# W's even rows in DMAs of 16 partitions instead of one of 64, and two pieces of the start's loads re-queued

## The chip, the cores and the metric

One NeuronCore of a Trainium2 chip runs the whole program. The metric is device time in microseconds (us). A time is the median of several executions; a run is called slow when it is over 1.5% above the fastest of the same kernel. "Span" is the profiled part of one execution; here it is about 1.7 us shorter than the time of that execution. A DMA is a transfer that the DMA engines carry out after some engine has issued it; "issued" and "landed" are the times of its issue and of the last increment of its semaphore in the trace. A call is one set of runs on one chip; the calls used different chips.

## The reference

Two branches of the same x [2048, 512] are mixed by a gate. Branch a is a spectral filter, branch b a two-layer network with Mish.

```python
x = A_x
g = sigmoid((x * gate_w).sum(-1, keepdims=True))
a = irfft2(rfft2(x) * (w_r + 1j * w_i))          # w_r, w_i: [2048, 257]
b = einsum(mish(einsum(x, w1) + b1), w2)         # w1: [512, 1792], w2: [1792, 512]
return g * a + (1 - g) * b
```

## The kernel before

The kernel is a list of tasks (one group of matmuls, one eviction, one DMA) that a list scheduler in the kernel file puts into one fixed order per engine when the program is built. In this program each engine then works through its own list in that order and waits at semaphores where it needs another's result.

TensorE's work, roughly in order: warm matmuls on zeros, transposes of x (L586), two stages of the spectral transform (L625, L636) interleaved with the first layer (L821, `mm1`), then the second layer (L843, `mm2`), the spectral middle with W (L761, L790), and the inverse stages (L870, L888). Between the stages the spectral data goes through DRAM twice: "shuffle writes" (`scr<-R`) and "shuffle reads" (`R<-scr`). The tile called hsb holds Mish results, and at first also the raw W (`SW`).

```python
def dma(name, dst, src, nbytes, reads=(), writes=(), deps=(), ..., queue="sp", ...):   # L465 is the issue
    ...
NWARM = 15
dma("ld_b1", ..., queue="act")
ld_x(0, 2); ld_w1(0); ld_x(2, 4); ld_w1(1)        # x on SyncE's queue; w1 pieces 0 and 1 on ScalarE's
ld_c(0, ...); ld_w1(2); ld_x(4, 8); ...           # SyncE's queue

def wload(w, src_t, deps=()):                     # w_r: 0, w_i: 1
    S_ = SW[:, w, :, :]
    row = S_.ap[0][0]
    G_ = (128 * 257, 16)
    # even partitions: 64 partitions, each one run of 16*257 elements (8224 bytes)
    S2 = bass.AP(S_.tensor, S_.offset, [[2 * row, 64], [1, 16 * 257]])
    part(0, S2, src(0, (16 * 257, 4), G_, (1, 16 * 257)), 64 * 8224, 300e3)   # source: 4 x 16 x 4112
    # odd partitions: 16 partitions each, rows of 257 elements (514 bytes), in reverse
    for bb in (0, 2, 1, 3):
        part(1 + bb, dst(...), src(..., G_, (-257, 16 - e0), (1, 257)), ...)
    part(5, ...)

wload(0, A_w_r)
ld_w2(0)
... # first stages; the four shuffle writes r1w
wload(1, A_w_i, t_e2)                             # t_e2: the evictions of L636
dma("ld_sm", SM[:], ...)                          # constants of the spectral middle
ld_w2(1, t_e2)
... # eight shuffle reads r1r
```

## Time and profile before

| | before |
|---|---|
| time, median of 3 | 141.91 us (141.03 to 142.57) |
| span of the profiled execution | 142.1 us |
| TensorE busy | 127.5 us, 90% |
| VectorE, ScalarE busy | 68%, 63% |

The execution that was profiled took 143.79 us, 1.9 more than this median.

From the page of the kernel before: span, TensorE's busy time, and three rows that cut the span into 40 slices of 3.55 us (busy share of TensorE, granted TensorE clock, busy share of the DMA engines, all in tenths).

```profile
span 142.1 us, 2309 instructions
PE 127.5 (90%) x800; PEld 68.4 (48%) x814; DVE 96.7 (68%) x213; ACT 89.0 (63%) x146; POOL 4.3 (3%) x8
...
PE   6574899999999906999999999999999999999992
...
PEclk9999999999999997799999999999999999999999
DMA  3999937999942896973446007210399722221021
```

TensorE is full from the sixth slice to the last, but for one hole (the 0 and the 6 near 50 us). In the slice of the 6 and in the one after it the clock is down to seven tenths. From 39 to 46 us, ahead of the hole, the DMA engines are only four and two tenths busy.

The waits of TensorE in the kernel before (what it waited for: total us, times, longest):

```profile
PE ps L843 <- DMA w_sb<-in_B_w_dram: 4.6, 1, 4.6
PE ps L821 <- DMA w_sb<-in_B_w_dram: 4.1, 2, 2.2
PE ps L508 <- DVE GD L505: 1.1, 1, 1.1
```

The hole is a wait for w2 (4.6 us). The 4.1 us are two waits for pieces of w1 at the start. TensorE's timeline shows where the hole falls: the second layer starts with w2's first half, and the second half is needed after 28 matmuls (one record is missing in the trace):

```profile
43.73 6.21 PE L843 MATMUL ps<-w_sb,hsb 128*128 128x512 bf16 x27
54.58 4.88 PE L843 MATMUL ps<-w_sb,hsb 128*128 128x512 bf16 x14 [4.65 <-DMA w_sb<-in_B_w_dram]
```

The timeline of SyncE's DMA queue in the kernel before (start us, length us of the issues, what, count):

```profile
16.18 6.10 SPq L465 DMA_DIRECT2D hsb<-in_A_w_r_dram  x6
22.32 1.49 SPq L465 DMA_DIRECT2D w_sb<-in_B_w_dram  x1
23.86 5.32 SPq L465 DMA_DIRECT2D SM<-c_sm  x1
29.36 4.00 SPq L465 DMA_DIRECT2D scr<-R  x4
33.41 11.81 SPq L465 DMA_DIRECT2D hsb<-in_A_w_i_dram  x6
45.27 0.59 SPq L465 DMA_DIRECT2D w_sb<-in_B_w_dram  x1
46.87 12.66 SPq L465 DMA_DIRECT2D R<-scr  x8
```

The six w_i issues took 11.81 us, although most issues take 0.6 to 0.8 us: the last one alone took 7.77 us. Only then, at 45.27 us, could w2's second half be issued. It landed at 54.54 us.

Windows of the kernel before (stretch; then TensorE busy, its weight loads, VectorE, ScalarE, GpSimd; last three columns: granted clock, DMA share, GB/s; the share adds up the times of packets, and these overlap, so it passes 1: 1.20 in the last row):

```profile
40.00:44.00 4.00, 4.00 (x21) 1.82 (x19) 3.80 (x10) 3.12 (x6) 1.78 (x1) 1.00 0.28 106
44.00:50.00 6.00, 5.88 (x27) 2.49 (x26) 5.40 (x10) 4.49 (x3) 1.74 (x1) 1.00 0.68 170
50.00:56.00 6.00, 1.42 (x5) 0.61 (x6) 2.96 (x5) 3.41 (x2) 0.00 (x0) 0.93 0.78 172
56.00:60.00 4.00, 4.00 (x15) 1.60 (x14) 0.28 (x1) 1.65 (x3) 0.00 (x0) 0.68 1.20 233
```

In 40 to 44 us the DMA share is 0.28, about 4 engines of 16, while a load that TensorE needs has not even been issued. That fits a transfer that uses few engines.

### The profile page before, as it was taken

To read this page: it belongs to the slowest core of one execution; us is meant where nothing else is said; L and a number is where in the kernel's file an instruction comes from. 1 tells how busy PE (TensorE), PEld (TensorE's weight loads), DVE (VectorE), ACT (ScalarE), POOL (GpSimd) and SP (SyncE) were. 2 spreads that over 40 slices of the span, in tenths; PEclk is the share of its full clock that TensorE was granted. 3 is DMA by queue.
4 is the path that set the end of the run, shared out by engine and by line. 5 is a ranking of instruction groups with operands and counts; after the bars stand their busy time and mean duration, and the time that the engine had idled before them with its cause. 6 is when DMAs were issued, how large, how long until landed. Compare 5 with 4: busy or idle time off the path is not lost.

```text
span 142.1 us, 2309 instructions
## 1 busy us (share of the span) xinstructions
PE 127.5 (90%) x800; PEld 68.4 (48%) x814; DVE 96.7 (68%) x213; ACT 89.0 (63%) x146; POOL 4.3 (3%) x8
## 2 busy tenths in 40 slices
PE   6574899999999906999999999999999999999992
PEld 4354767664444402444344354444445665665451
DVE  0512849779999835199999999995003899799422
ACT  0333987998888728436495878896886665875000
POOL 2000000000018000000000000000000000000000
PEclk9999999999999997799999999999999999999999
DMA  3999937999942896973446007210399722221021
GB/s 101 322 401 405 257 90 115 166 175 326 392 151 95 212 213 152 227 123 86 99 109 187 1 0 294 105 51 24 141 237 217 123 91 110 95 81 74 2 109 37
DMA packets 33136, 22.01 MB, mean 155 GB/s; under 512 B 24037, under 2 KB 29413, under 8 KB 32997
## 3 DMA queue, kind: packets, MB, share of 16 engines
q1 hardware_dynamic: 32040, 21.35, 57.9%
q10 hardware_dynamic: 1084, 0.53, 1.3%
q8 instruction: 6, 0.10, 0.3%
q14 instruction: 6, 0.04, 0.1%
HBM read 14.00 MB, written 6.29 MB: 143 GB/s over the span
## 4 chain that ended last, share of the span: by engine, by line
PE 47%; DVE 21%; DMA 14%; SPq 8%; issue 4%; ACT 3%; ACTq 1%; DVEq 0%
PE ps L843 20%; PE ps L821 16%; DMA w_sb<-in_B_w_dram 14%; SPq L465 8%; DVE PX L775 4%; DVE PX L774 4%; DVE PX L771 3%; DVE PX L778 3%; PE ps L888 3%; PE ps L870 3%; ACT R L491 2%; DVE R L490 2%; PE ps L625 2%; DVE WW L669 2%; PE ps L636 1%
## 5 line engine op out<-in xcount | busy, mean ns | idle before, releaser
L843 PE MATMUL ps<-w_sb,hsb 128*128 128x512 bf16 (+2 forms) x231 | 52.6, 375 | 5.0 <-DMA w_sb<-in_B_w_dram 4.6
L821 PE MATMUL ps<-xT,w_sb 128*128 128x512 bf16 (+1 forms) x233 | 52.8, 369 | 4.9 <-DMA w_sb<-in_B_w_dram 4.1
L830 ACT ACTIVATE hsb<-ps,b1f 128x512 bf16<-128x512 f32 (+1 forms) x60 | 38.4, 662 | 11.1 <-PE ps L821 11.0
L843 PEld LDWEIGHTS ps<-w_sb,hsb 128*128 128x128 bf16 x238 | 22.7, 100 | 29.2 <-DMA w_sb<-in_B_w_dram 5.1
L821 PEld LDWEIGHTS ps<-xT,w_sb 128*128 128x128 bf16 x240 | 23.0, 99 | 28.1 <-issue 2.6
L490 DVE CAST R<-ps 128x512 bf16<-128x512 f32 (+1 forms) x22 | 14.6, 687 | 7.6 <-PE ps L625 5.7
L491 ACT ACTIVATE R<-ps 128x512 bf16<-128x512 f32 (+1 forms) x26 | 14.5, 594 | 4.2 <-PE ps L625 2.5
L854 ACT ACTIVATE R<-ps,omg 128x512 bf16<-128x512 f32 x12 | 8.2, 686 | 8.5 <-PE ps L843 8.5
L491 ACT ACTIVATE PX<-ps 128x512 bf16<-128x512 f32 x15 | 8.9, 595 | 4.7 <-DVE PX L775 2.3
L666 ACT ACTIVATE WW<-hsb 32x2080 bf16<-32x2080 bf16 x4 | 7.8, 1938 | 4.1 <-DMA hsb<-in_A_w_i_dram 3.8
L665 DVE COPY WW<-hsb 32x2080 bf16<-32x2080 bf16 x12 | 8.4, 696 | 2.7 <-DMA hsb<-in_A_w_i_dram 2.4
L677 DVE SCALAR_TENSOR_TENSOR R<-R,gwb 128x512 bf16<-128x512 bf16 x16 | 9.9, 685 | 0.3 <-ACT R L491 0.3
L895 ACT ACTIVATE PX<-ps,gcol 128x256 f32<-128x256 f32 x14 | 6.3, 472 | 4.6 <-PE ps L888 4.6
L877 DVE CAST TT<-ps 128x512 bf16<-128x512 f32 x3 | 2.0, 688 | 9.9 <-PE ps L870 9.9
L778 DVE TENSOR_TENSOR PX<-PX 128x512 bf16<-128x512 bf16 x16 | 6.8, 423 | 0.8
L880 ACT ACTIVATE TT<-ps 128x512 bf16<-128x512 f32 x13 | 7.3, 595 | 0.0
L774 DVE TENSOR_TENSOR PX<-PX,WW 64x512 bf16<-64x512 bf16 x16 | 6.7, 421 | 0.5
L775 DVE TENSOR_TENSOR PX<-PX,WW 64x512 bf16<-64x512 bf16 x16 | 6.7, 419 | 0.2
L771 DVE TENSOR_TENSOR PX<-PX,WW 128x512 bf16<-128x512 bf16 x16 | 6.7, 420 | 0.2
L916 DVE SCALAR_TENSOR_TENSOR R<-ps,omg,R 128x512 bf16<-128x512 f32 (+2 forms) x5 | 3.2, 642 | 4.9 <-PE ps L843 4.9
L904 DVE SCALAR_TENSOR_TENSOR PX<-ps,gcol,PX 128x256 bf16<-128x256 f32 x12 | 5.7, 478 | 0.7 <-ACT PX L895 0.7
L790 PE MATMUL ps<-PX,SM 128*128 128x512 bf16 x15 | 5.7, 382 | 0.4 <-DVE PX L778 0.3
(72 smaller groups left out, 97.8 us busy)
## 6 DMA issues: line engine op xcount, KB each, us to landing
scr<-R SPq DMA_DIRECT2D x8, 512.0 KB, 6.8
R<-scr SPq DMA_DIRECT2D x16, 256.0 KB, 5.0
w_sb<-in_B_w_dram SPq DMA_DIRECT2D x2, 896.0 KB, 11.6
out_dram<-R SPq DMA_DIRECT2D x7, 256.0 KB, 2.0
R<-in_A_x_dram SPq DMA_DIRECT2D x3, 512.0 KB, 10.7
w_sb<-in_B_w_dram SPq DMA_DIRECT2D x1, 1280.0 KB, 8.9
hsb<-in_A_w_r_dram SPq DMA_DIRECT2D x1, 514.0 KB
hsb<-in_A_w_i_dram SPq DMA_DIRECT2D x1, 514.0 KB
```

Source lines behind the costliest of these rows:

```text
L465: start = (lambda e: e.dma_start_transpose(dst, src)) if transpose else (lambda e: e.dma_start(dst, src))
L490: t = G.add(name, [("dve", dve_dur(n), lambda e: e.tensor_copy(out=outf(), in_=inf())), ("act", act_dur(n), lambda e: e.activation(outf(), ...
L491: ("act", act_dur(n), lambda e: e.activation(outf(), inf(), AF.Copy))],
L665: t_wc.append(G.add(f"wv{w}{bb}{v}", [("dve", dve_dur(2080, 4), lambda e, wv=wv: e.tensor_copy(**wv())), ("act", act_dur(2080), lambda e, ...
L677: t_gx.append(G.add(f"gx{t}", [("dve", 0.72, lambda e, t=t: e.scalar_tensor_tensor(out=x_sb[:, t, :], in0=x_sb[:, t, :], scalar=1.0, in1=g ...
L771: return e.tensor_tensor(out=v(P1, sP, 0, 128), in0=v(Xb, sX, 0, 128), in1=Wa[:, js, 0:128], op=ALU.mult)
L774: e.tensor_tensor(out=v(P2, sQ, 0, 64), in0=v(Xb, sX, 64, 128), in1=Wb[64:128, js, 0:128], op=ALU.mult)
L775: return e.tensor_tensor(out=v(P2, sQ, 64, 128), in0=v(Xb, sX, 0, 64), in1=Wb[0:64, js, 0:128], op=ALU.mult)
L778: return e.tensor_tensor(out=P1[:, sP.i, :], in0=P1[:, sP.i, :], in1=P2[:, sQ.i, :], op=ALU.add)
L821: ins = e.matmul(ps[:, bk(sl), cols], w1_sb[:, dt_, 128 * ft:128 * (ft + 1)], xT[:, dt_, 4 * c + h0:4 * c + h1, :], start=(dt_ == 0), stop ...
L830: return e.activation(hsb[:, hb, ft, cols], ps[:, bk(sl), cols], AF.Mish, bias=b1f[:, ft:ft + 1])
L843: ins = e.matmul(ps[:, bk(sl), 0:n1 - n0], hsb[:, hb, ft, 128 * tl:128 * (tl + 1)], w2_sb[:, ft, n0:n1], start=(ft == 0), stop=(ft == NFT ...
```

## The change

Its intent: W's even rows should use all DMA engines; w1's second piece should not be late; the constants should not stand ahead of the first shuffle's writes. Numbers of the scheduler's model were changed as well, so the order of all engines was computed anew. Cut to its core:

```diff
-NWARM = 15
+NWARM = 20
-XBAR_BW = 95e3
+XBAR_BW = 270e3
...
-            t = G.add(name, [(queue, {"sp": 0.46, "act": 0.46, "pool": 1.0}[queue], start)],
+            t = G.add(name, [(queue, 1.3 if transpose else 0.46, start)],
...
-            ... queue="act" if h < 2 else "sp", prio=199.5 - 2 * h if h < 2 else None)
-
-        dma("ld_b1", ..., queue="act", prio=202.0)
-        ld_x(0, 2, bw=400e3)
+            ... queue="sp" if h else "act", prio=None if h else 199.5)
+
+        ld_x(0, 2, bw=250e3)
         ld_w1(0)
-        ld_x(2, 4)
+        dma("ld_b1", ..., queue="act", prio=198.5)
+        G.tasks[-1].lat = 0.8
+        ld_x(2, 4, bw=290e3)
         ld_w1(1)
...
-            S2 = bass.AP(S_.tensor, S_.offset, [[2 * row, 64], [1, 16 * 257]])
-            part(0, S2, src(0, (16 * 257, 4), G_, (1, 16 * 257)), 64 * 8224, 300e3)
             for bb in (0, 2, 1, 3):
                 e0 = 0 if bb else 1
+                part(6 + bb, bass.AP(S_.tensor, S_.offset + 32 * bb * row, [[2 * row, 16], [1, 16 * 257]]), src(16 * bb, G_, (1, 16 * 257)), 16 * 8224, 220e3)
                 part(1 + bb, dst(32 * bb + 1, 16, e0, 16 - e0), ...)
...
         wload(1, A_w_i, t_e2)
-        dma("ld_sm", SM[:], ...)
         ld_w2(1, t_e2)
+        dma("ld_sm", SM[:], ..., deps=t_e2)
```

More of the change, by code (lines that the diff above doesn't have):

```diff
@@ L209 @@
     __slots__ = ("name", "opts", "eng", "dur", "fn", "deps", "pools", "prio", "idx", "isdma", "xfer",
-                 "sem", "semval", "sig", "start", "done", "nleft", "succ", "bias")
+                 "lat", "sem", "semval", "sig", "start", "done", "nleft", "succ", "bias")
 class _Slot:
@@ L248, in add @@
         t.isdma = False
-        t.xfer = t.bias = 0.0
+        t.xfer = t.bias = t.lat = 0.0
         t.sem, t.semval, t.sig = None, 0, 0
@@ L356, in schedule @@
                 bw_free = xs + t.xfer
-                t.done = bw_free + 0.9
+                t.done = bw_free + 0.9 + t.lat
             else:
@@ L520, in ld_w1 @@
         def ld_w1(h):
-            f0, f1, bw = ((0, 256, 250e3), (256, 512, 280e3), (512, F, 370e3))[h]
-            dma(f"ld_w1_{h}", w1_sb[:, :, f0:f1], w1v[:, :, f0:f1], 128 * 4 * 2 * (f1 - f0), writes=[("w1", h)], bw=bw, queue="act" if h < 2 else "sp", prio=199.5 - 2 * h if h < 2 else None)
-        dma("ld_b1", bgraw[0:14, :], B_b1.rearrange("(ft p) -> ft p", p=128), 3584, writes=["braw"], queue="act", prio=202.0)
-        ld_x(0, 2, bw=400e3)
+            f0, f1, bw = ((0, 256, 290e3), (256, 512, 290e3), (512, F, 370e3))[h]
+            dma(f"ld_w1_{h}", w1_sb[:, :, f0:f1], w1v[:, :, f0:f1], 128 * 4 * 2 * (f1 - f0), writes=[("w1", h)], bw=bw, queue="sp" if h else "act", prio=None if h else 199.5)
+        ld_x(0, 2, bw=250e3)
         ld_w1(0)
-        ld_x(2, 4)
+        dma("ld_b1", bgraw[0:14, :], B_b1.rearrange("(ft p) -> ft p", p=128), 3584, writes=["braw"], queue="act", prio=198.5)
+        G.tasks[-1].lat = 0.8
+        ld_x(2, 4, bw=290e3)
         ld_w1(1)
@@ L649, in _build @@
         wload(1, A_w_i, t_e2)
-        dma("ld_sm", SM[:], d_c["SM"][:], 128 * 2 * 128 * len(MATS), writes=["SM"])
         ld_w2(1, t_e2)
+        dma("ld_sm", SM[:], d_c["SM"][:], 128 * 2 * 128 * len(MATS), writes=["SM"], deps=t_e2)
         t_wc = []
@@ L666, in _build @@
                                             ("act", act_dur(2080), lambda e, wv=wv: e.activation(wv()["out"], wv()["in_"], AF.Copy))],
-                          reads=[("S", w, 0), ("S", w, 1 + bb)] + [("S", w, 5)] * (not bb), writes=[("W", w, v, bb)], deps=t_e2, prio=PR["cp"]))
+                          reads=[("S", w, 6 + bb), ("S", w, 1 + bb)] + [("S", w, 5)] * (not bb), writes=[("W", w, v, bb)], deps=t_e2, prio=PR["cp"]))
             for h in range(2):
```

## The prediction

> **What bounds it now.** TensorE: the page's first part has it 90% busy (127.5 of 142.1 us), and the timeline shows dense matmuls from 12.7 us to 139.4 us with one hole. The waits view names its idle time: 4.6 us for w2's second half (the hole, 49.9 to 54.6 us), 4.1 us for two pieces of w1 at the start (2.2 us up to 8.0, 1.9 us up to 12.7), 1.1 us for the first memset. After the hole the granted clock is 0.68 in 56 to 60 us (windows view; the clock records have one half-speed stretch of 3.4 us), so about 1.7 us more are lost there.
>
> **Why the hole.** Each W load starts with one DMA whose source has an outer dimension of 4. [...] that DMA's semaphore gets four late increments (30.6 to 30.9 us for w_r, 47.2 to 49.0 for w_i). Every later transfer shows 12 increments early and 4 late: w2's first half 30.9 to 32.1 against 36.0 to 36.2 us, the w_i pieces 38 to 40 against 47 to 52. The mean DMA share meanwhile is 0.28 to 0.45 (40 to 48 us). SyncE's queue stalls behind it: one w_i issue took 7.77 us (37.5 to 45.3), so w2's second half was issued only at 45.3 and landed at 54.5; the shuffle reads ran 46.9 to 63.1.
>
> **The change.** The 514 KB DMA becomes four of 16 partitions, which should use all 16 engines. It costs 6 more issues at 0.6 to 0.9 us on SyncE's queue, which has the time. Expected order: last shuffle write, nine w_i DMAs, w2's second half, constants, eight shuffle reads. Estimate: last shuffle write issued near 32 us, nine issues of 0.7 us to 38.3, w2's second half landed near 42 to 43 us, constants near 44, shuffle reads (1.2 us each, as now) done near 53 to 54 instead of 63. TensorE needs the second half at about 48: the hole (4.65) and its slow clock (1.7) go. Gate products and W copies keep VectorE until about 54, so its middle phase ends near 89 instead of 97, and the second shuffle moves with it.
>
> At the start, w1's second piece on ScalarE's queue landed on its last engine at 12.6 us although half had landed at 8.3; behind x 2-3 on SyncE's queue it should land near 7 to 8. b1 behind w1's first piece costs nothing (first use 9 us). The 1.9 us wait goes; the 2.2 us one shrinks by 0 to 1; five more warm matmuls fill idle time. Estimate 2 us.
>
> **Sum.** 142 - 4.65 - 1.7 - 2 = 133.6 us; I add 1.4 us for new small waits in the fixed order: 135.0 us, range 132.3 to 138.8. Chances: faster 0.88, same 0.10, slower 0.02.
>
> **What would show it.** No 4-late pattern in W's landings; no issue over 3 us after 30 us; no TensorE wait on w2 over 1 us; full clock in 50 to 60 us; first shuffle's reads done by 55; no w1 wait near 12 us; TensorE's busy share 93 to 95%.
>
> **What would make it wrong.** The shuffle reads overtake w2's second half (the hole stays); a shuffle write waiting on SyncE holds up W's pieces; short rows set W's time; VectorE's middle phase becomes the limit and TensorE waits for it or for the second shuffle.

142 - 4.65 - 1.7 - 2 = 133.6, and 1.4 for new waits, make the 135.0 us. That DMAs of 16 partitions would use all 16 engines was only my expectation then; what the runs show of it stands below, under "How many engines a DMA used".

## The result

| | before | after |
|---|---|---|
| time, median of 4 | 141.47 us (140.75 to 142.57) | 133.12 us (133.04 to 133.44) |
| span of the profiled execution | 142.1 us | 131.7 us |
| TensorE busy | 127.5 us, 90% | 126.1 us, 96% |
| w2's second half issued / landed | 45.27 / 54.54 us | 33.58 / 42.55 us |
| first matmul of the second layer | 43.73 us | 39.39 us |
| first shuffle's reads done | 63.07 us | 53.73 us |

The kernel is faster: ratio 0.9408, 95% interval 0.9338 to 0.9477. A ratio here is the mean time of one kernel's fast runs over that of the other's of the same rounds, so it is not quite the ratio of the medians.

The page of the kernel after, the same rows (slices of 3.29 us):

```profile
span 131.7 us, 2348 instructions
PE 126.1 (96%) x819; PEld 67.9 (52%) x819; DVE 94.9 (72%) x211; ACT 90.3 (69%) x149; POOL 4.3 (3%) x8
...
PE   6998999999999999999999999899999999999991
...
PEclk9999999999999999999999999999999999999999
DMA  3999989999999999134493212039992224002211
```

TensorE is full from the second slice on, the hole and the low clock are gone, and the DMA engines are busy almost without a break until 53 us. TensorE's waits after (the same view; the three longest):

```profile
PE ps L508 <- DVE GD L505: 1.1, 1, 1.1
PE ps L636 <- ACT R L491: 0.6, 1, 0.6
PE ps L790 <- DVE PX L778: 0.5, 1, 0.5
```

No wait for w1 or w2 is left in this list. But the new order asks for w2's second half after 14 matmuls of the second layer, not 28:

```profile
39.39 7.91 PE L843 MATMUL ps<-w_sb,hsb 128*128 128x512 bf16 x35
```

The fifteenth of these is the first that needs the second half. It was due at about 42.4 us, the half landed at 42.55, and it ran at 42.59. So the hole is closed with nothing to spare. SyncE's queue after:

```profile
17.22 1.33 SPq L465 DMA_DIRECT2D hsb<-in_A_w_r_dram  x2
18.73 0.46 SPq L465 DMA_DIRECT2D scr<-R  x1
19.25 4.60 SPq L465 DMA_DIRECT2D hsb<-in_A_w_r_dram  x7
23.89 0.58 SPq L465 DMA_DIRECT2D w_sb<-in_B_w_dram  x1
24.63 2.77 SPq L465 DMA_DIRECT2D scr<-R  x3
27.44 6.10 SPq L465 DMA_DIRECT2D hsb<-in_A_w_i_dram  x9
33.58 0.58 SPq L465 DMA_DIRECT2D w_sb<-in_B_w_dram  x1
34.21 1.35 SPq L465 DMA_DIRECT2D SM<-c_sm  x1
36.59 12.89 SPq L465 DMA_DIRECT2D R<-scr  x8
```

Nine w_i issues now take 6.10 us, where six took 11.81. Windows after, the same stretches:

```profile
40.00:44.00 4.00, 3.98 (x19) 1.68 (x18) 3.71 (x9) 3.67 (x3) 0.27 (x1) 1.00 1.15 328
44.00:50.00 6.00, 6.00 (x31) 2.75 (x30) 5.30 (x8) 5.93 (x6) 0.00 (x0) 1.00 1.22 217
50.00:56.00 6.00, 6.00 (x31) 2.81 (x30) 5.71 (x11) 2.64 (x5) 0.00 (x0) 1.00 0.51 98
```

In 40 to 44 us the DMA engines move 328 GB/s instead of 106.

**How many engines a DMA used** I read from the increments of its semaphore, which the trace records one by one. These are the times (us) of the increments, copied from the traces; the first line of each pair is W's even rows, the second w2's first half, issued after them.

```
before   w_r, 64 partitions, issued 16.18:  17.32 | 30.62 30.64 30.65 30.85
before   w2 first half, issued 22.32:       30.95 31.18 31.19 31.22 31.24 31.33 31.39 31.41 31.68 31.77 31.78 32.06 | 36.02 36.05 36.10 36.23
after    w_r, last quarter, issued 21.93:   sixteen increments, 25.18 to 27.34
after    w2 first half, issued 23.89:       sixteen increments, 29.63 to 31.24
```

The 64-partition DMA has one early record and four late ones, at 30.62 to 30.85 us. w2's first half, issued 6 us later, has twelve increments by 32.06 us and four about 4 us later (36.02 to 36.23). I read this as four engines that carried W's even rows and were still behind. The trace does not name engines: that a late increment stands for one engine, and that they are the same four, is inferred. The packets fit. W's even rows are the only packets of 8224 bytes in the trace. In the kernel before at most 6 of them were under way at once (on average 3.9 for w_r and 3.5 for w_i), in the kernel after up to 16 for w_r and 12 for w_i (on average 6.5 and 6.7). The source was 4 x 16 x 4112 before; a quarter has 16 on both sides, and the last of w_r has sixteen increments within 2.2 us. So in these two kernels the number followed the source's outer dimension; why it does is not shown. The lag does not last for ever: in the kernel before, the third shuffle read (issued at 51.65 us) has all its sixteen increments within 56.73 to 57.41, so the prediction's "every later transfer" goes too far.

**The start.** TensorE's timeline before, then after (the length of a group shows the clock):

```profile
8.04 1.01 PE L821 MATMUL ps<-xT,w_sb 128*128 128x256 bf16 x4 [2.19 <-DMA w_sb<-in_B_w_dram]
8.84 1.06 PE L586 MATMUL ps<-ident,R 128*128 128x128 bf16 x8
9.70 1.06 PE L821 MATMUL ps<-xT,w_sb 128*128 128x256 bf16 x4
12.66 0.61 PE L821 MATMUL ps<-xT,w_sb 128*128 128x256 bf16 x4 [1.91 <-DMA w_sb<-in_B_w_dram]
```

```profile
6.27 0.62 PE L586 MATMUL ps<-ident,R 128*128 128x128 bf16 x8
6.73 1.54 PE L821 MATMUL ps<-xT,w_sb 128*128 128x256 bf16 x12
8.11 1.06 PE L625 MATMUL ps<-CF,R 128*128 128x128 bf16 x16
9.00 0.60 PE L821 MATMUL ps<-xT,w_sb 128*128 128x256 bf16 x4
```

Four matmuls of 128x256 take 1.01 us at 8 us in the kernel before and 0.60 in the kernel after: before, TensorE still ran at half speed (its first full-speed record begins at 10.75 us, after at 5.92). The windows view prints a clock of 1.00 there, since no record covers that stretch; the durations tell. In this pair of executions the second layer starts 4.34 us earlier (43.73 to 39.39): 1.31 from the first matmul of layer one (8.04 to 6.73), 1.91 from the second wait, less 0.23 for a longer wait on ScalarE (0.39 to 0.62), and 1.35 left over, which fits the three groups that ran at half speed (0.41 + 0.44 + 0.46).

### The profile page after: what moved, and what is told of

Its sections match the earlier page's. It is cut to its first block, busy times and chain, and to the rows that moved or that the text cites. A ratio compares the mean times of both kernels' runs of the same rounds, so it can differ in the third digit from the quotient of the medians.

```text
span 131.7 us, 2348 instructions
## 1 busy us (share of the span) xinstructions
PE 126.1 (96%) x819; PEld 67.9 (52%) x819; DVE 94.9 (72%) x211; ACT 90.3 (69%) x149; POOL 4.3 (3%) x8
## 4 chain that ended last, share of the span: by engine, by line
PE 88%; DVE 6%; ACT 2%; issue 1%; DVEq 0%
PE ps L843 36%; PE ps L821 32%; PE ps L508 3%; PE ps L870 3%; PE ps L888 3%; PE ps L625 2%; PE ps L636 2%; PE ps L790 2%; PE ps L761 2%; DVE PX L775 1%; DVE PX L774 1%; ACT R L491 1%; ACT hsb L830 1%; PE ps L586 1%; DVE PX L778 1%
## 5 line engine op out<-in xcount | busy, mean ns | idle before, releaser
L821 PE MATMUL ps<-xT,w_sb 128*128 128x512 bf16 (+1 forms) x240 | 52.1, 365 | 0.2 <-ACT hsb L830 0.2
L843 PE MATMUL ps<-w_sb,hsb 128*128 128x512 bf16 (+2 forms) x238 | 51.6, 366 | 0.0
L491 ACT ACTIVATE R<-ps 128x512 bf16<-128x512 f32 (+1 forms) x29 | 16.2, 597 | 2.1 <-PE ps L790 0.8
L490 DVE CAST R<-ps 128x512 bf16<-128x512 f32 (+1 forms) x19 | 12.5, 686 | 5.9 <-PE ps L625 3.4
## 6 DMA issues: line engine op xcount, KB each, us to landing
hsb<-in_A_w_r_dram SPq DMA_DIRECT2D x7, 128.5 KB, 4.4
hsb<-in_A_w_i_dram SPq DMA_DIRECT2D x7, 128.5 KB, 8.0
```

Source lines behind the costliest of these rows:

```text
L490: t = G.add(name, [("dve", dve_dur(n), lambda e: e.tensor_copy(out=outf(), in_=inf())), ("act", act_dur(n), lambda e: e.activation(outf(), ...
L491: ("act", act_dur(n), lambda e: e.activation(outf(), inf(), AF.Copy))],
L821: ins = e.matmul(ps[:, bk(sl), cols], w1_sb[:, dt_, 128 * ft:128 * (ft + 1)], xT[:, dt_, 4 * c + h0:4 * c + h1, :], start=(dt_ == 0), stop ...
L843: ins = e.matmul(ps[:, bk(sl), 0:n1 - n0], hsb[:, hb, ft, 128 * tl:128 * (tl + 1)], w2_sb[:, ft, n0:n1], start=(ft == 0), stop=(ft == NFT ...
```

## The experiments

Twelve kernels. In all but the last one of them the order of instructions on every engine was kept as in the kernel it starts from; only what the edit names was moved or replaced, after the scheduler had run. Without that, each edit would have made a new order and mixed two causes. All twelve gave correct results. The program that compares fast runs calls b_quarters, a_w1act and a_b1first faster, a_whole and b_w1sp the same, and the other seven unclear: in the second and third call the kernel before scattered from 139.5 to 145.9 us (and once took 341). Where it says unclear, I compare the times themselves, across calls; the kernel after and its variants without a hole took 132.8 to 134.6 us in every call. Theory A (4 engines being the reading of the increments above): the 64-partition DMA runs on 4 engines, and their backlog holds up SyncE's queue and w2's second half. Rival B: the gain comes from the new order.

### b_quarters: the kernel before, with the quarters alone

```diff
 order = G.schedule()
+for w in range(2):            # replace ld_W{w}0 in SyncE's list by four quarters,
+    ...                       # each just ahead of its short-row piece; readers wait on their own quarter
```

> The kernel before, every engine's order of instructions kept; only each W's 64-partition DMA is replaced by four of 16 partitions, each issued just ahead of its own short-row piece. Theory A (the 64-partition DMA runs on 4 of the 16 DMA engines, and their backlog holds up SyncE's queue and with it w2's second half): w2's second half lands by 44 us instead of 54.5, the hole at 50 us and the half-speed clock after it go, about 135.5 us (6 us less than before; 134.5 to 136.5). Rival B (the gain comes from the new order: constants moved back, other interleaving): no more than 1 us is gained, 140.5 us or more.

Measured: 134.74 us (before: 142.10), ratio 0.9497, interval 0.9444 to 0.955. w2's second half landed at 43.43 us; there is no wait for w2, and the clock record shows no half-speed stretch. The largest wait left is w1's:

```profile
PE ps L823 <- DMA w_sb<-in_B_w_dram: 3.3, 2, 2.6
```

Theory A holds, and B is out as the main cause: with the old order and the constants in their old place, the quarters alone give most of the gain.

### a_whole: the kernel after, with the 64-partition DMAs put back

```diff
 order = G.schedule()
+for w in range(2):            # the first quarter's task issues all 64 partitions, the other three are dropped
+    ...
```

> The kernel after, every engine's order kept; only the four 16-partition DMAs of each W are put back into one of 64 partitions at the place of the first. Theory A: four late semaphore increments return, w2's second half is issued several us later than 33.6 and lands near 50, TensorE, which now comes to it at 42.5 us, waits 6 to 9 us and loses up to 1.7 us of clock after it: 140 to 143 us. Rival B (order): within 1 us of the kernel after, 133 to 134.

Measured: fast runs 142.88 and 143.21 us (two more, slow, 145.2), ratio to before 1.0087. So the whole gain is lost, at the upper end of what A expected or just above it. The profiled run is one of the slow ones; its longest wait and its queue:

```profile
PE ps L845 <- DMA w_sb<-in_B_w_dram: 9.4, 1, 9.4
```

```profile
33.11 10.89 SPq L465 DMA_DIRECT2D hsb<-in_A_w_i_dram  x5
44.05 0.59 SPq L465 DMA_DIRECT2D w_sb<-in_B_w_dram  x1
```

The long issue is back. The half landed at 52.00 us, 2.5 us earlier than in the kernel before, and yet TensorE waits longer, because it asks for it 7.3 us earlier (42.60 instead of 49.93): 4.3 from the earlier start of the second layer and 3.0 from the new order. A half-speed stretch of 10.24 us begins inside the hole and ends 5.1 us after it.

### a_halves: two DMAs of 32 partitions

```diff
+# as a_whole, but two DMAs per W: source (16*257, 2), (128*257, 16), (1, 4112); 32 partitions each
```

> The kernel after, every order kept; the even rows of each W in two DMAs of 32 partitions (source outer dimension 2) instead of four of 16. [...] each runs on 2 engines, so each of the two carries 257 KB per W, twice what each of four carried; w2's first half is late too (needed at 39.4 us, landed near 46 on those two), its second half near 60: 148 to 160 us, worse than one DMA of 64 partitions (142.9 to 145.2). Rival (cutting the DMA into smaller ones is what helps, whatever engines they take): between the kernel after and that, 134 to 142 us.

That an outer dimension of 2 means 2 engines was my expectation, from the 4 of the kernel before.

Measured: 153.48 us, ratio 1.0902. w2's first half has 14 increments by 32.23 us and 2 at 38.33 and 39.32; its second half landed at 60.44.

```profile
PE ps L845 <- DMA w_sb<-in_B_w_dram: 17.9, 1, 17.9
```

This is the sharpest test. Halving the DMA made it 10 us slower than not cutting it, and the increments go with it: the source's outer dimension fell from 4 to 2, and the late increments of w2's first half from 4 to 2. So the smaller size alone does not help; what the quarters have besides is the 16 in the outer dimension. One DMA of all 64 partitions with a 16 outermost was not tried. (The two kernels ran in different calls; their ratios, 1.0902 and 1.0087, say the same.)

### a_whole_r and a_whole_i: one of the two W's put back

```diff
-for w in range(2):
+for w in (0,):                # a_whole_r; (1,) in a_whole_i
```

> The kernel after, every order kept; only w_r's even rows go back to one DMA of 64 partitions, w_i stays in quarters. Theory A: four engines fall 6 to 8 us behind in w_r, stay behind through w2's first half and the shuffle writes (as when both were whole: 38.4 and 42.1 us), and catch up little before w2's second half: it lands at 47 to 49 us instead of 42.6, a hole of 5 to 6 us [...]: 139 to 141.5 us.

> The kernel after, every order kept; only w_i's even rows go back to one DMA of 64 partitions, w_r stays in quarters. Theory A: 218 KB per slow engine stand between the last shuffle write (35.0 us) and the end of w2's second half, at about 24 KB a us (8224 bytes took 311 to 339 ns in the kernel before) some 9 us: landing near 45.5 us, a hole of about 3 us: 136 to 138.5 us. With w_r's loss added this should come near the 10 us that both cost together.

(What the 139 to 141.5 us expected of a_whole_r has beyond 133.12 and a hole of 5 to 6 was allowed for half speed after the hole; the 3.41 us of half speed in the kernel before are worth 1.7.)

Measured, fast runs: a_whole_r 140.31 and 141.01 us; a_whole_i 137.84, 138.50 and 139.75. In the profiled runs (both slow by the 1.5% rule) w2's second half landed at 49.50 and 47.93 us, with holes of 7.2 and 5.5 us. Each W alone costs, w_r more although it is loaded 11 us earlier: the lag it leaves is not made up in time (w2's second half has twelve increments by 45.84 us and four from 46.70 to 49.50).

The increments also part the two delays that theory A joins, the late issue and the engines' lag. In the kernel before, w2's second half was issued at 45.27 us and had twelve increments by 52.06 and the last at 54.54: most of its delay is the late issue, and the lag adds 2.5 us. In a_whole_i its issue began at 33.57, as early as in the kernel after (33.58; it took 3.56 us, though, not 0.58). Twelve increments came by 44.36 and the last at 47.93, against 42.55 in the kernel after: here the lag makes 3.6 us of the 5.4.

By time, a_whole_r came out as expected (139 to 141.5), while one fast run of a_whole_i (139.75) lies above its 136 to 138.5. Its landing was expected near 45.5 and came 2.4 us later in the profiled run. The rate assumed was too high for that run: w_i's packets of 8224 bytes had a median of 311 ns in the kernel before (with some up to 615; those of w_r 630), and 528 ns in a_whole_i. Whether the two costs add up is open. Over the kernel after they are about 7.5 and 5.5 us against 9.9 for both by the times of fast runs, but these are of different calls; by each call's ratio to the kernel before they are 6.3 and 4.3 against 9.6, which nearly add up.

### b_w1sp: the kernel before, w1's second piece on SyncE's queue

```diff
+q = find("ld_w1_1"); order["act"].remove(q)
+order["sp"].insert(order["sp"].index(find("ld_x2")) + 1, q)
```

> The kernel before, every order kept; only w1's second piece moves from ScalarE's queue to SyncE's, behind x 2-3. Theory C (on ScalarE's queue its packets are served last, that alone makes it late): it lands near 7 to 8 us instead of 12.6, the 1.9 us wait goes, and the wait for w1's first piece shrinks as its queue has no second tenant; 2 to 3 us less than before, 138.5 to 139.5, unless the hole at 50 us takes the gain back: w2's second half does not come earlier, so then 141 to 142. I hold the second for likelier: the hole absorbs it (hole near 7 us instead of 4.65). Rival (it is late because of its 512-byte rows, on whichever queue): it still lands after 10 us.

Measured: fast runs 143.43, 143.59 and 144.00 us, ratio 1.0131: no gain, rather a loss of 1%, where 141 to 142 us was expected. (That packets on ScalarE's queue are served last was my theory; no run tests it.) The piece landed at 7.08 us instead of 12.62 and TensorE reached the second layer at 40.53 instead of 43.73, but w2's second half landed at 54.03, as before:

```profile
PE ps L843 <- DMA w_sb<-in_B_w_dram: 7.3, 1, 7.3
...
PE ps L821 <- DMA w_sb<-in_B_w_dram: 0.8, 1, 0.8
```

The hole took back 2.7 of the 3.2 us (4.65 to 7.34), as I had held for likelier. The half-speed stretch doubled, from 3.41 to 6.83 us, but it begins at 51.01 us, inside the hole, so only 3.8 us of it fall on matmuls, about as much as before. What makes the 1% is not shown. A gain ahead of a wait for something that is late anyway was worth nothing here.

### a_w1act: the kernel after, w1's second piece back on ScalarE's queue

```diff
+q = find("ld_w1_1"); order["sp"].remove(q); q.eng = "act"
+order["act"].insert(order["act"].index(find("ld_b1")) + 1, q)
```

> The kernel after, every order kept; only w1's second piece goes back to ScalarE's queue, behind b1. Theory C: it lands between 10 and 12.6 us instead of 6.7, TensorE, which needs it third, waits from about 8 to 12 us, and nothing later absorbs it: 3 to 4 us more, 136 to 137 us. Rival (the start was won by b1's place and by warm matmuls): within 1 us of the kernel after.

Measured: 133.21 us, ratio 0.9398: no loss at all. I was wrong about this one. The piece did land late (9.41 us instead of 6.71, though not as late as the 10 to 12.6 expected), but in the new order TensorE first runs three groups on w1's first piece, L625, another group and L636, and asks for the second piece only at 11.17 us (in the kernel after). Here the order protects.

### bq_w1sp: quarters and the moved piece, in the old order

```diff
+# b_quarters and b_w1sp together
```

> The kernel before, every order kept, with W's rows in quarters and w1's second piece on SyncE's queue behind x 2-3: the two together. If the move is worth nothing by itself (as it was when undone in the kernel after): 134.7 as with the quarters alone. If it is worth its wait once the hole is gone: the 2.6 us wait at 7.8 us goes, 132.4 to 133.2 us, as fast as the kernel after.

Measured: two kinds of runs, 132.26 and 132.86 us (fast) and 134.75 and 134.77 (slow by the 1.5% rule). The fast ones are about 2 us below b_quarters (134.74, of another call), the slow ones as slow as it, and the verdict is unclear. So the move may be worth its wait once the hole is gone; two runs without a trace do not show it. The one profiled is a slow one: in it w1's first piece landed at 7.03 us, TensorE waited 1.58 us for it, and the full clock began at 10.51 us, as in the kernel before; in b_quarters it began at 5.65. Whether a late clock makes the difference between the two kinds is not shown, since no fast run was profiled. Its best runs are the fastest of all, but half of its runs are not, so it does not beat the kernel after.

### a_smearly, a_warm15, a_b1first: the three small parts, undone one at a time

```diff
+# a_smearly: ld_sm moved behind ld_w2_0, without its dependencies
+# a_warm15:  warm15 to warm19 removed from TensorE's list
+# a_b1first: ld_b1 moved ahead of ld_w1_0 on ScalarE's queue
```

> The kernel after, every order kept; only the load of the constants goes back to its old place on SyncE's queue, behind w2's first half. Theory A: with all engines sharing the load nothing near it is short of time; w2's second half lands no later, 132.6 to 133.8 us. Rival B in its weaker form (its place matters): 1 us or more slower.

> The kernel after, every order kept, without the last five of the 20 warm matmuls. If they bring the clock up early: [...] 1 to 2 us more. If the clock comes up anyway [...]: within 0.3 us. I hold the second for a little likelier, as the half-speed record of the kernel with W in quarters and 15 warm matmuls also ended at 5.65 us.

> The kernel after, every order kept; only b1's load goes back ahead of w1's first piece on ScalarE's queue. w1's first piece is then issued at 1.5 instead of 0.8 us and lands at 6 to 8 us (as in the kernels with the old order: 6.2 to 7.9) instead of 5.1 to 5.3; TensorE waits up to 1.5 us for it [...]: 133.3 to 135, with more scatter than the kernel after. If b1's place is worth nothing: 133.0 to 133.5.

Measured: a_smearly 133.51 us (133.41 to 134.59), a_warm15 133.44 (133.09 to 133.90), a_b1first 133.44 (132.79 to 133.82), against 133.12 for the kernel after. By these medians each part is worth 0.4 us at most, about what the runs scatter. In the profiled run of a_smearly, its slowest, w2's second half landed 1.1 us later (43.69) and TensorE waited 1.25 us for it, so the place of the constants can cost something. That wait also shows the missing slack: over the kernel after and the five variants of it without a hole, w2's second half landed from 41.30 to 43.69 us, and TensorE asks for it at about 42.4. With b1 first, w1's first piece landed at 6.42 us, and TensorE did not wait for it, because the transposes of x run first in the new order; that expectation of mine failed. Without the last five warm matmuls the full clock began at 5.70 us, with them at 5.92, so in these runs the five added nothing. The transposes and the first 15 left no gap over 0.64 us after the first matmul; whether that is what counts for the clock was not tested.

### a_fill: an attempt at something better

```diff
+q = find("mm1_0_2_0"); order["pe"].remove(q)
+order["pe"].insert(order["pe"].index(find("a1_0")), q)
```

> The kernel after with one group of four matmuls (the third F tile's first half) moved ahead of the second group of stage 1, so that it fills the 0.62 us that TensorE waits for ScalarE's eviction at 9.6 us. All later orders kept. TensorE is busy from there to the end, so 0.4 to 0.6 us should come off: 132.4 to 132.8 us. If something else sets the pace: 133.1.

Measured: 133.11 us (132.98 to 133.60), no gain. The 0.62 us wait shrank to 0.17, but 0.21 us came up two groups later, TensorE reached the second layer at 39.25 us instead of 39.39, and the rest is within the scatter.

## Why the prediction was right

The prediction was 135.0 us in 132.3 to 138.8; measured were 133.12.

- **"Why the hole"**: shown. Four engines, as I read the increments; b_quarters removes the hole, a_whole brings it back, a_halves makes it worse, with two late increments. The late issue is most of the delay in the kernel before, the lag of the four engines the rest (2.5 us).
- **"the hole (4.65) and its slow clock (1.7) go"**: both gone. Measured by itself (b_quarters), the quarters are worth 7.1 us (0.0503 of 141.47), against 6.35 predicted.
- **"TensorE needs the second half at about 48"**: wrong for the kernel after, and it came out well by luck. It holds for the old order (b_quarters asks at 47.49 us and has the half at 43.43). The new order, which the change computed anew, asks at about 42.4, and the half landed at 42.55. Of the 5 to 6 us of slack in the prediction none was there; a landing 1.1 us later already made a wait of 1.25 us (a_smearly).
- **"Estimate 2 us" for the start**: the profiled pair shows 4.34 us. That pair overstates it: the profiled execution of before took 143.79 us, 2.3 more than the median, and its first w1 piece landed at 7.90 us, where the same order gave 6.17 in b_quarters and 6.27 in b_w1sp. Between b_quarters and the kernel after, the second layer starts 2.05 us earlier (41.44 to 39.39) and the time is 1.6 us shorter, close to the 2 us; but these two kernels differ in everything else of the change too, so no run measures the start by itself. What I left out of the sum was the half-speed run at 8 to 10.7 us, in full view in the durations.
- **"The 1.9 us wait goes"** for the reason given ("behind x 2-3 on SyncE's queue it should land near 7 to 8 us"): it landed at 6.71, and it went, but in the new order it would have gone on the old queue too (a_w1act). In the old order the queue is what counts: in b_w1sp the move alone brought the piece to 7.08 us and the wait was gone. The change holds two remedies for one wait.
- **"I add 1.4 us for new small waits"**: this is the term that was mis-sized. The new waits are 0.62 and 0.46 us, and others of the old kernel went with them. TensorE's busy share came to 96%, not 93 to 95. Without the 1.4 us the prediction's own sum was 133.6; the kernel took 133.12.
- **Order and times on the queue**: the order was as written. w2's second half landed at 42.55 ("near 42 to 43"), the constants at 43.85 ("near 44"), the shuffle reads at 53.73 ("near 53 to 54"). But two errors cancel in these times. The last shuffle write was issued at 26.7, not "near 32" (in the kernel before a constants' issue of 5.32 us stood ahead of the writes; with the quarters alone it was 29.45; start and order gave the rest), and so w2's second half was issued at 33.58 instead of 38.3. It then took 9.0 us to land instead of the 3.7 to 4.7 that the prediction allowed, while the DMA engines still had earlier transfers to do (the last write landed at 35.0, the last piece of w_i at 40.3; DMA share 0.96 from 20 to 30 us and 1.09 from 30 to 40). So I put the landing down to the bytes ahead of it, not to the issues that the prediction counted. VectorE's middle phase ended at 84.1, not "near 89", so the second shuffle gained more than predicted. One issue after 30 us took 3.50 us, against "no issue over 3 us": a shuffle read in a queue full of them, and nothing waited for it.

## What to carry to other kernels

Read the outer dimension of both sides of every DMA (W's even rows had 64 in the destination and 4 in the source). Here loads with 4 or 2 outermost in the source left 4 or 2 late increments on transfers behind them in the queue (w2's first half: 36.02 to 36.23 us in the kernel before, 38.33 and 39.32 in a_halves), even on one issued 11.9 us later (w2's second half, after w_i's even rows: twelve increments by 52.06 us, the last at 54.54). In these profiles its signs were a DMA share near a quarter (0.25 to 0.28 from 40 to 44 us in the kernel before, a_whole and a_halves) and one issue of 5 to 8 us (an issue of 3.5 us also occurs in the kernel after, without harm). But a_whole_r has a share of 0.97 in that stretch and still a hole of 7.2 us, so the late increments are the surer sign. Then find the last wait first: with the hole in place, a start that was 3 us better gained nothing. And when a scheduler computes the order anew, look up again when each load is needed: here that moved by 5 us.

## What else the runs show

- The number of increments went with the outer dimension in every case here (4, 2 and 16 for outer dimensions 4, 2 and 16; b1's load of 14 rows shows 14 and one early record). Behind the DMAs with few, later DMAs of the queue were late for a time: w2's first half landed at 28.8 to 31.2 us without them and 36.2 to 39.3 with them, w2's second half at 41.3 to 44.0 and 47.9 to 60.4. Issues became long meanwhile (7.77 us for one; how the one causes the other was not tested).
- One transfer of 514 KB was slower than four of 128.5 KB by 5% of the kernel's time (0.9497 for the four), and in the new order two of 257 KB were slowest (1.0902, against 1.0087 for one).
- w1's second piece (256 KB in 512-byte rows) landed at 9.4 to 12.6 us on ScalarE's queue beside SyncE's loads of 2 to 4 KB rows, and at 6.6 to 7.2 us on SyncE's. What makes the difference was not tested.
- The half-speed stretches that go with holes of 4.65, 5.5, 7.2, 7.3, 9.4 and 17.9 us (all but the first begin inside the hole) were 3.41, 6.83, 10.24, 6.83, 10.24 and 20.48 us, whole multiples of 3.41; what sets their length is not shown. In the profiled execution of the kernel before, three groups at half speed at the start cost 1.31 us, 0.9% of it. In bq_w1sp, with no hole at all, runs fell into two groups 1.7% apart, and the one profiled in the slow group had its full clock at 10.51 us, where b_quarters had it at 5.65; but b_quarters was as slow (134.74 against 134.75), so that the late clock makes the 1.7% is not shown.
- A single profile can be an unlucky one. The kernel before took 139.5 to 145.9 us over all its runs (and once 341), with a mean clock of 0.953 to 1.0, which does not by itself order the times; the kernel after stayed within 0.4 us in its four runs.
